# Fourier filter and gated convolution on one core: mixing by three real products for a pair of tiles, and the 64-point transform back in float32 quarters

## The chip, the cores and the metric

The kernel runs on one core of one Trainium2 chip. The core has a matrix engine (TensorE, PE in the profile, with its weight loads as PEld), a vector engine (VectorE, DVE), a scalar engine (ScalarE, ACT), GpSimd (POOL), and queues of DMA transfers that SyncE (SP) issues here. The metric is the device time of one execution in microseconds. A profiled execution has a span, from its first to its last instruction, and a time of its own, a little longer.

## The reference

```python
X = np.fft.rfft(x, axis=1)                 # x: 8 x 3200 x 256
Yr = Xr @ w_r - Xi @ w_i + b_r             # w_r, w_i: 256 x 256
Yi = Xr @ w_i + Xi @ w_r + b_i
Y = soft_threshold(Yr, 0.01) + 1j * soft_threshold(Yi, 0.01)
y = np.fft.irfft(Y, n=3200, axis=1)
gate = sigmoid(causal convolution of y, 5 taps per channel)
out = (gate * (y @ w_val)) @ w_out         # w_val, w_out: 256 x 256
```

The two sums Yr and Yi are a complex product of each frequency's 256 channels with a 256 x 256 matrix. They are called the mixing below.

## The kernel before

The 3200 positions are taken as 64 x 50, so that the long transform becomes a 50-point transform (p1 in the code), a 64-point one with its twiddles (s2), the mixing, the soft threshold, the 64-point transform back (s1i) and the 50-point transform back (s2i). Between p1 and s2, and between s1i and s2i, the data go to DRAM and come back in another layout. Then, for eight blocks of a batch, the gated convolution follows: value product v, five taps and the sigmoid, gate, output product o.

After s2 a batch has 25 tiles of 128 frequencies' real and imaginary parts. They are worked on in 12 pairs and a last single tile (u counts them, 13 for each batch). For a pair:

- s2 (L556) makes the spectrum of both tiles in PSUM (s, one buffer): float32 matmuls with the constants f2.
- ACT copies it to the type fp32r, which PE multiplies in one pass (L566, high part); DVE subtracts that from the spectrum (L568, low part); ACT negates the imaginary half (L571). So xs holds a high and a low part of [-Xi, Xr, Xi].
- The mixing (L591, L592) sums, for each of the two tiles, 2 halves of the channels x 3 products of high and low parts x 2 (real matrix, imaginary matrix) = 12 matmuls of 128 x 128 by 256 columns in PSUM (y_ps, one buffer): 24 for the pair.
- DVE adds the bias (L607, yb), ACT and DVE apply the threshold (L612, L614, tp), ACT and DVE split the result in high and low parts again (r_hl, by the helper at L311 and L313).
- s1i (L639) transforms back by 3 matmuls a tile, in fp32r with split constants g1, to PSUM (z_ps, one buffer of its own); ACT copies that (L646) and SP stores it.

The 50-point transforms (p1 at L517, y_p at L693) are float32 matmuls in four 64 x 64 quarters of PE, which run side by side.

What the engines do when is fixed ahead of time. Every step is added to a plan with an engine, an assumed duration, what it reads and writes, and a due time: `at` plus an offset from the table O. The plan (class Plan) is a list scheduler: it takes, piece by piece, the one of earliest due time among those that could begin soonest, with assumed costs for a change between quarters and full-width work (SWITCH) and a bound on the buffers of each kind (SLOTS). The result is one fixed order on each engine's queue. PSUM is given out by SLOTS too: one buffer each for the spectrum, the mixing and z, and two of two banks (ps_2), which p1, s2i, v and o share.

Of the kernel before, what the change touches and what calls it, by code (L numbers as in the profile page):

```python
# [32 lines left out]
def dft_constants():  # L33
# [46 lines left out]
class Plan:  # L80
# [11 lines left out]
    def add(self, at, engine, busy, fn, uses=(), sets=(), new=None, delay=None, quarters=False, kb=0, chain=None):  # L92
# [10 lines left out]
        p = dict(n=n, at=at, engine=engine, busy=busy, fn=fn, before=before, new=new or {}, quarters=quarters, kb=kb,  # L103
# [7 lines left out]
    def order(self):  # L111
# [25 lines left out]
        in_quarters, wire = False, 0.0  # L137
# [13 lines left out]
        while len(done) < len(pieces):  # L151
            best = None
            for e in engines:
# [56 lines left out]
SWITCH = 88  # L210
# [11 lines left out]
def act(n, kind="copy"):  # L222
# [36 lines left out]
def fourier_filter_then_gated_conv(ctx: ExitStack, tc: tile.TileContext, x, w_r, w_i, b_r, b_i,  # L259
# [57 lines left out]
    def load_matrix(at, name, w, dst):  # L317
# [52 lines left out]
    def load_matrix64(at, name, w, dst, uses=()):  # L370
# [23 lines left out]
    def load_g1(at, part):  # L394
        t = slice(part * 5, part * 5 + 5)
        key = ("st_g1", part)
        n = 5 * P

        def load():
            st = room(key, "g_hl", n).rearrange("p (t q) -> p t q", t=5)  # L400
            nc.sync.dma_start(out=st, in_=g1[:, t, :])
        add(at, "SP", 400, load, STORED, [key + (0,)], {key: "g_hl"}, kb=320)
        split(at + 0.01, n, ("g1", part), lambda: tl[key][:, 0:n].rearrange("p (t q) -> p t q", t=5),
              lambda: g1_sb[:, 0, t, :], lambda: g1_sb[:, 1, t, :], [key + (0,)])

    def load_bias(at):

        def load():
            for k, rows in ((0, N1), (1, N1 + 1)):
                for lo, hi, b in ((0, rows, b_r), (rows, P, b_i)):  # L410
                    nc.sync.dma_start(out=bias_sb[lo:hi, k, :],
                                      in_=b.rearrange("(o d) -> o d", o=1).to_broadcast([hi - lo, D]))
        add(at, "SP", 2200, load, STORED, [("bias", 0, 0)], kb=256)

    def load_bias_rows(at):
        key = ("b_hl", 0)
        v = lambda k: tl[key].rearrange("p (a d) -> p a d", a=2)[:, k, :]
        hl = split(at, D, key, lambda: bias_sb[:, 0, :], lambda: v(0), lambda: v(1), [("bias", 0, 0), ("a_dram", B - 2, 7)], {key: "tp"},
                   lambda: room(key, "tp", 2 * D, F32R))

        def rows():
            nc.vector.memset(f32(bias_hl[:, :]), 0.0)
            for row, k in ((0, 0), (32, 1), (64, 0), (96, 1)):
                nc.vector.tensor_copy(out=bias_hl[row:row + 1, :], in_=f32(v(k)[row:row + 1, :]))
            nc.vector.memset(f32(sel_sb[:, :]), 0.0)
            for row in range(0, P, 32):
                nc.vector.memset(f32(sel_sb[row:row + 1, row // N1 * N1:row // N1 * N1 + N1]), 1.0)
        add(at + 0.01, "DVE", 2500, rows, [*hl, ("a_dram", B - 2, 7)], [("bias_hl", 0, 0)])
# [463 lines left out]
```

## Time and profile before

| | us |
|---|---|
| median of 3 runs (lowest, highest) | 937.63 (937.32, 938.09) |
| the profiled execution's own time | 938.27 |
| its span | 936.5 |
| PE busy | 901.2 |
| weight loads (PEld) busy | 806.0 |
| DVE busy | 739.3 |
| ACT busy | 671.5 |

An engine's busy time is the union of its instructions' records. PE's records overlap, since matmuls are pipelined, so a busy PE says that it was never out of work, and not how long one matmul takes; for that one reads from one start to the next. The granted clock of PE was 0.985 of full speed on average. The timelines and groups that the prediction uses are shown there. In all of them a float32 matmul has two records (and two weight loads), a matmul in fp32r one.

### The profile page before, as it was taken

The page shows a single profiled execution, that of the slowest core. Times are in us where ns is not written, and L with a number is a line of the kernel's source. Part 1 is how long each engine was busy: PE and PEld are TensorE (multiplying, and loading weights), DVE is VectorE, ACT ScalarE, POOL GpSimd, SP SyncE. Part 2 cuts the span into 40 slices and gives each one's busy share as a digit, 9 for nine tenths or more (in the row PEclk, how much of TensorE's full clock was granted, in tenths as well). Part 3 has the DMA queues.
Part 4 walks back from the last instruction along what each step waited for, and adds up shares of the span by engine and source line. Part 5 has one row for each costly group of instructions (what it writes and reads, how often), then busy time and mean ns, then how long its engine had stood idle before and what let it go on. Part 6 is the DMA issues. An engine that isn't in the chain of part 4 may idle for free.

```text
span 936.5 us, 23789 instructions
## 1 busy us (share of the span) xinstructions
PE 901.2 (96%) x9918; PEld 806.0 (86%) x9918; DVE 739.3 (79%) x1211; ACT 671.5 (72%) x1091; POOL 3.7 (0%) x8
## 2 busy tenths in 40 slices
PE   7799699999999999999999999999999999999897
PEld 2488678899889998999889998899988999999675
DVE  1155776889778896898787895989878988988896
ACT  1176467878778777878777786878777787776664
POOL 0000000000000000000000000000001000000000
PEclk9699899999999999999999999999999999999999
DMA  6687666745675357644676356653664444422612
GB/s 202 211 256 238 182 211 207 234 152 164 206 230 183 99 187 245 218 135 142 204 224 215 114 170 210 221 162 124 213 231 152 134 155 134 146 88 76 196 70 87
DMA packets 105232, 164.52 MB, mean 176 GB/s; under 512 B 10054, under 2 KB 78406, under 8 KB 105126
## 3 DMA queue, kind: packets, MB, share of 16 engines
q1 hardware_dynamic: 104166, 159.74, 53.6%
q10 hardware_dynamic: 960, 3.28, 1.0%
q8 instruction: 78, 1.28, 0.6%
q14 instruction: 28, 0.23, 0.1%
HBM read 84.34 MB, written 78.64 MB: 174 GB/s over the span
## 4 chain that ended last, share of the span: by engine, by line
PE 67%; DVE 21%; ACT 5%; DMA 4%; issue 2%; SPq 1%; ACTq 0%; DVEq 0%
PE y_ps L591 12%; PE y_ps L592 12%; DVE acc L754 10%; PE o_ps L725 10%; PE v_ps L725 9%; PE s L556 8%; PE z_ps L639 7%; PE y_p L693 5%; PE p L517 5%; DVE acc L766 2%; DVE gated L313 2%; DVE yb L607 2%; DMA x<-in_x 1%; DVE xs L568 1%; DVE y_hl L313 1%
## 5 line engine op out<-in xcount | busy, mean ns | idle before, releaser
L754 DVE SCALAR_TENSOR_TENSOR acc<-y_sb,cw_sb,acc 128x400 f32<-128x400 f32 x512 | 300.5, 632 | 4.4 <-ACT acc L751 3.8
L591 PE MATMUL y_ps<-wri_sb,xs 128*128 128x256 f32 x1200 | 296.4, 287 | 2.0 <-DVE yb L607 1.2
L592 PE MATMUL y_ps<-wri_sb,xs 128*128 128x256 f32 x1152 | 277.5, 281 | 5.9 <-ACT xs L571 5.9
L591 PEld LDWEIGHTS y_ps<-wri_sb,xs 128*128 128x128 f32 x1200 | 227.4, 189 | 11.0 <-issue 5.9
L592 PEld LDWEIGHTS y_ps<-wri_sb,xs 128*128 128x128 f32 x1152 | 218.9, 190 | 6.1 <-ACT xs L571 6.1
L725 PE MATMUL o_ps<-gated,wo_sb 128*128 128x400 f32 x756 | 151.2, 348 | 0.0
L725 PEld LDWEIGHTS o_ps<-gated,wo_sb 128*128 128x128 f32 x756 | 134.5, 188 | 2.8
L725 PE MATMUL v_ps<-y_hl,wv_sb 128*128 128x400 f32 x636 | 127.2, 346 | 0.7 <-ACT r_hl L311 0.7
L556 PEld LDWEIGHTS s<-f_sb,a 128*128 128x128 f32 x800 | 101.8, 193 | 26.1 <-DVE xs L568 11.6
L556 PE MATMUL s<-f_sb,a 128*128 128x128 f32 x800 | 112.1, 282 | 9.0 <-DVE xs L568 4.8
L725 PEld LDWEIGHTS v_ps<-y_hl,wv_sb 128*128 128x128 f32 x636 | 112.3, 188 | 0.9 <-ACT r_hl L311 0.9
L566 ACT CAST xs<-s 128x512 fp32r<-128x512 f32 (+1 forms) x104 | 59.1, 568 | 56.6 <-PE y_ps L592 39.4
L313 DVE TENSOR_TENSOR r_hl<-tp,r_hl 128x512 fp32r<-128x512 f32 (+1 forms) x103 | 68.6, 666 | 35.2 <-ACT r_hl L311 34.9
L639 PE MATMUL z_ps<-r_hl,g_sb 128*128 128x256 f32 x594 | 93.9, 290 | 0.5 <-DVE r_hl L313 0.2
L607 DVE TENSOR_TENSOR yb<-y_ps,bias_sb 128x512 f32<-128x512 f32 (+1 forms) x103 | 68.5, 665 | 32.4 <-PE y_ps L592 31.9
L639 PEld LDWEIGHTS z_ps<-r_hl,g_sb 128*128 128x128 f32 x594 | 80.5, 189 | 13.2 <-ACT gated L311 3.2
L612 ACT ACTIVATE tp<-yb,nlam 128x512 f32<-128x512 f32 (+1 forms) x103 | 72.5, 705 | 23.3 <-DVE yb L607 20.9
L764 ACT ACTIVATE acc<-acc 128x400 f32<-128x400 f32 x128 | 67.1, 536 | 29.6 <-DVE acc L754 29.1
L311 ACT CAST gated<-acc 128x800 fp32r<-128x800 f32 x63 | 54.3, 862 | 45.3 <-DVE acc L766 45.1
L568 DVE TENSOR_TENSOR xs<-s,xs 128x512 fp32r<-128x512 f32 (+1 forms) x104 | 69.2, 665 | 18.1 <-ACT xs L566 18.1
L614 DVE SCALAR_TENSOR_TENSOR tp<-yb,tp 128x512 f32<-128x512 f32 (+1 forms) x103 | 68.6, 666 | 18.6 <-ACT tp L612 18.5
L751 ACT ACTIVATE acc<-y_sb,cw_sb 128x400 f32<-128x400 f32 x128 | 75.8, 628 | 9.7 <-DVE gated L313 9.7
(70 smaller groups left out, 944.5 us busy)
## 6 DMA issues: line engine op xcount, KB each, us to landing
zl<-z_dram SPq DMA_DIRECT2D x128, 200.0 KB
out<-o SPq DMA_DIRECT2D x63, 400.0 KB
a<-a_dram SPq DMA_DIRECT2D x96, 256.0 KB
z_dram<-z_t SPq DMA_DIRECT2D x96, 256.0 KB
x<-in_x SPq DMA_DIRECT2D x120, 200.0 KB
a_dram<-s SPq DMA_DIRECT2D x120, 200.0 KB
x<-in_x ACTq DMA_DIRECT2D x8, 200.0 KB
f_sb<-in_f SPq DMA_DIRECT2D x5, 320.0 KB
```

The source lines that it names most:

```text
L313: add(at + 0.001, "DVE", dve(n), lambda: nc.vector.tensor_tensor(out=low(), in0=src(), in1=f32(high()), op=ALU.subtract), [*uses, hl[0]], ...
L556: nc.tensor.matmul(p[:, 2 * i + c, :], tl[ka][:, i, c * P:(c + 1) * P], f2_sb[:, t, :], start=True, stop=True)
L568: add(at + O["s2"] + 0.1, "DVE", dve(m * P), lambda: nc.vector.tensor_tensor(out=xs()[:, 0:m, 1, N1:], in0=tl[k2][:, 0:m, :], in1=f32(xs() ...
L591: nc.tensor.matmul(p[:, i, :], xr, wri_sb[:, 0, hw, c, :], start=k == 0, stop=False)
L592: nc.tensor.matmul(p[:, i, :], xi, wri_sb[:, 1, hw, c, :], start=False, stop=k == 5 and not late)
L607: nc.vector.tensor_tensor(out=buffer(kb, "yb", [P, 2, D])[:, 0:n], in0=tl[ky][:, 0:n], in1=b_, op=ALU.add)
L612: nc.scalar.activation(out=buffer(kt, "tp", [P, 2, D])[:, 0:n], in_=src()[:, 0:n], func=AF.Relu, bias=nlam)
L614: add(at + 0.2, "DVE", dve(n * D), lambda: nc.vector.scalar_tensor_tensor(out=tl[kt][:, 0:n], in0=src()[:, 0:n], scalar=LAM, in1=tl[kt][:, ...
L639: nc.tensor.matmul(p[:, i, :], g1_sb[:, hg, t, :], tl[kr][:, hr, i, :], start=k == 0, stop=k == 2)
L725: nc.tensor.matmul(p[:, e, 0:TB], w[:, hw, c, e * P:(e + 1) * P], src(hy, c), start=n == 0, stop=n == 5)
L751: nc.scalar.mul(block(acc(c)), y_at(k, c, 0), cw_sb[:, c, 0:1])
L754: nc.vector.scalar_tensor_tensor(out=block(acc(c)), in0=y_at(k, c, j), scalar=cw_sb[:, c, j:j + 1], in1=block(acc(c)), op0=ALU.mult, op1=A ...
```

## The change

Mixing. With K = (Xr + Xi) w_r the mixing becomes Yr = K - Xi (w_r + w_i) and Yi = K + Xr (w_i - w_r): three real products instead of four. Both tiles of a pair are put side by side, real parts of both in one block of 128 columns and imaginary parts in another, so that each product takes 2 x 3 matmuls for the pair: 6 for K (k_ps, L620), 12 for the other two (y_ps, L615), 18 instead of 24. The sum Xr + Xi (sx) is made in float32: ACT copies the imaginary part (L595), DVE adds the real part (L602); ACT and DVE split it (L606, L607). The spectrum itself is split as before (L599, L603), the negation goes. DVE adds the bias to K for both parts (L626), then adds the other two products (L629). The last single tile of a batch keeps the four products.

Transform back. The threshold's result tp is no longer split. s1i of a pair is 8 float32 matmuls of 64 x 64 quarters by 256 columns (L651), to a buffer of ps_2 and no longer to one of its own; the single tile takes one full-width float32 matmul (L644). g1 is laid out for it, loaded as it is, and no longer split at the start.

Order. The planner has costs for five kinds of changes on PE, and other offsets; a late pair of the last batch and its preparations are dropped; the assumed landing of two loads is later by 3 and 4 us.

```diff
-SWITCH = 88
+SWITCH = {"rq": 92, "fq": 174, "qr": 75, "qf": 75, "ff": 77}
-O = {'load_x': -2.458,
+O = {'load_x': -2.454,
...
-SLOTS = {"x": 3, "zl": 3, "y_hl": 2, "s1": 2, "r_hl": 2, "a": 3, "xs": 2, "xz": 1, "yb": 2, "tp": 2, "zst": 3,
-         "acc": 2, "g_hl": 2, "o": 2, "ps_s2": 1, "ps_y": 1, "ps_z": 1, "ps_2": 2, "a_dram": 2, "z_dram": 2}
+SLOTS = {"x": 3, "zl": 3, "y_hl": 2, "s1": 2, "a": 3, "xs": 2, "sx": 2, "xz": 1, "yb": 2, "tp": 2, "zst": 3,
+         "acc": 2, "g_hl": 2, "o": 2, "ps_s2": 1, "ps_y": 1, "ps_k": 2, "ps_2": 2, "a_dram": 2, "z_dram": 2}
...
+            add(at2, "ACT", act(D), imag, done, [kd_ + (0,)], {kd_: "sx"})
+            add(at2 + 0.001, "ACT", act(2 * D, "cast"), high, done, [kx + (0,)], {kx: "xs"})
+            add(at2 + 0.001, "DVE", dve(D), lambda: nc.vector.tensor_tensor(out=sx(), in0=spec()[:, :, 0], in1=sx(), op=ALU.add), done, [kd_ + (0,)])
+            add(at2 + 0.002, "DVE", dve(2 * D), lambda: nc.vector.tensor_tensor(
+                out=tl[kx][:, 512:1024], in0=tl[k2].rearrange("p a b -> p (a b)"), in1=f32(tl[kx][:, 0:512]), op=ALU.subtract),
+                [*done, kx + (0,)], [kx + (1,)])
+            add(at2 + 0.003, "ACT", act(D, "cast"), lambda: nc.scalar.copy(out=ss(0), in_=sx()), [kd_ + (0,)], [kx + (2,)])
+            add(at2 + 0.004, "DVE", dve(D), lambda: nc.vector.tensor_tensor(out=ss(1), in0=sx(), in1=f32(ss(0)), op=ALU.subtract),
+                [kd_ + (0,), kx + (2,)], [kx + (3,)])
...
-            for c in range(2):
-                for hx, hw in ((0, 0), (0, 1), (1, 0)):
-                    xr = xs()[:, 2 * i + c, hx, N1:]
-                    xi = tl[kq][:, c, hx, :] if last else xs()[:, 2 * i + c, hx, 0:P]
-                    nc.tensor.matmul(p[:, i, :], xr, wri_sb[:, 0, hw, c, :], start=k == 0, stop=False)
-                    nc.tensor.matmul(p[:, i, :], xi, wri_sb[:, 1, hw, c, :], start=False, stop=k == 5 and not late)
+                for r, m in ((1, 2), (0, 3)):
+                    for k, (c, hx, hw) in enumerate((c, *h) for c in range(2) for h in HL):
+                        nc.tensor.matmul(p[:, 1 - r, :], xm(hx, c, r), w_sb[:, m, hw, c, :], start=k == 0, stop=k == 5)
+            def mix_sum():
+                p = buffer(kk, "ps_k", [P, D])
+                for k, (c, hx, hw) in enumerate((c, *h) for c in range(2) for h in HL):
+                    nc.tensor.matmul(p, sm(hx, c), w_sb[:, 0, hw, c, :], start=k == 0, stop=k == 5)
+            def bias():
+                nc.vector.tensor_tensor(out=buffer(kb, "yb", [P, 2, D]), in0=tl[kk].rearrange("p (a d) -> p a d", a=1).to_broadcast([P, 2, D]),
+                                        in1=bias_sb[:, 0:2], op=ALU.add)
+            add(at + 0.2, "DVE", dve(2 * D), lambda: nc.vector.tensor_tensor(out=yb(), in0=tl[ky], in1=yb(), op=ALU.add), [ky + (0,)], [kb + (0,)])
...
-            rs = split(at + 0.21, n * D, kr, lambda: tl[kt][:, 0:n], lambda: tl[kr][:, 0, 0:n], lambda: tl[kr][:, 1, 0:n],
-                       [kt + (0,)], {kr: "r_hl"}, lambda: buffer(kr, "r_hl", [P, 2, 2, D], F32R))
...
-            for k, (hg, hr) in enumerate(((0, 0), (0, 1), (1, 0))):
-                nc.tensor.matmul(p[:, i, :], g1_sb[:, hg, t, :], tl[kr][:, hr, i, :], start=k == 0, stop=k == 2)
+            for r in range(2):
+                for i in range(2):
+                    for e in range(2):
+                        nc.tensor.matmul(p[e * HP:(e + 1) * HP, i, 0:D], g[i * HP:(i + 1) * HP, r, e * HP:(e + 1) * HP],
+                                         tl[kt][i * HP:(i + 1) * HP, r, :], start=r == 0, stop=r == 1)
```

Line numbers of the change (L595 to L656 and so on) are those of the kernel with the change.

More of the change, by code (lines that the diff above doesn't have):

```diff
@@ L90, in __init__, with add @@
         self.opened, self.last = {}, {}
-    def add(self, at, engine, busy, fn, uses=(), sets=(), new=None, delay=None, quarters=False, kb=0, chain=None):
+    def add(self, at, engine, busy, fn, uses=(), sets=(), new=None, delay=None, mode="r", kb=0, chain=None, extra=0):
         n = len(self.pieces)
@@ L136, in order @@
         free = {e: 0.0 for e in engines}
[L137 removed]
+        mode, wire = "r", 0.0
         done = []
@@ L394, in load_g1 @@
     def load_g1(at, part):
[L395 to L404, printed above, removed]
+        t = slice(part * 5 * P, (part + 1) * 5 * P)
+        add(at, "SP", 400, lambda: nc.sync.dma_start(out=g1_sb[:, t], in_=g1[:, t]), STORED, [("g1", part, 0)], kb=320)
     def load_bias(at):
         def load():
[L409 to L428, printed above, removed]
+            for k, lo, hi, b in ((0, 0, P, b_r), (1, 0, P, b_i), (2, 0, N1 + 1, b_r), (2, N1 + 1, P, b_i)):
+                nc.sync.dma_start(out=bias_sb[lo:hi, k, :], in_=b.rearrange("(o d) -> o d", o=1).to_broadcast([hi - lo, D]))
+        add(at, "SP", 2200, load, STORED, [("bias", 0, 0)], kb=384)
     def load_conv(at):
@@ L596, in p2, with mix @@
-        w = [("w", m_, h) for m_ in ("w_r", "w_i") for h in ("high", "low")]
-        for i in range(n):
-            add(at, "PE", 1404 + 117 * late, lambda i=i: mix(i), [*parts, *w, *([("bias_hl", 0, 0)] if late else [])],
-                [ky + (i,)] + ([("turn", "mix", u)] if b == 0 and i == 0 else []), {ky: "ps_y"} if i == 0 else None)
-        made = [ky + (i,) for i in range(n)]
-        if late:
-            src, us = (lambda: tl[ky]), made
-        else:
+            def mix():
+                p = buffer(ky, "ps_y", [P, 2, D])
+                for k, (c, hx, hw) in enumerate((c, *h) for c in range(2) for h in HL):
+                    nc.tensor.matmul(p[:, 0, :], xs()[:, c, hx, N1:], w_sb[:, 0, hw, c, :], start=k == 0, stop=False)
+                    nc.tensor.matmul(p[:, 0, :], tl[kq][:, c, hx, :], w_sb[:, 1, hw, c, :], start=False, stop=k == 5)
@@ L645, in keep @@
+        add(at + O["s1i"], "PE", 430 if last else 900, s1i, [kt + (0,), *gs], [kz + (0,)], {kz: "ps_2"}, mode="f" if last else "q")
         def keep():
-            nc.scalar.copy(out=buffer(ko, "zst", [P, 2, D])[:, 0:n], in_=tl[kz][:, 0:n])
+            nc.scalar.copy(out=buffer(ko, "zst", [P, 2, D])[:, 0:n], in_=tl[kz][:, 0:n, 0:D])
         def store():
```

204 lines of the change are left out of this document (107 added, 97 removed).

## The prediction

> **What bounds the kernel now.** I read the page's busy line and chain of waits first, then the table of windows for one batch.
>
> ```profile
> span 936.5 us, 23789 instructions
> PE 901.2 (96%) x9918; PEld 806.0 (86%) x9918; DVE 739.3 (79%) x1211; ACT 671.5 (72%) x1091; POOL 3.7 (0%) x8
> PE 67%; DVE 21%; ACT 5%; DMA 4%; issue 2%; SPq 1%; ACTq 0%; DVEq 0%
> ```
> Two rows of the chain in order of time (start, length):
>
> ```profile
> 434.83 2.73 DVE acc L754 x5
> 543.24 2.73 DVE acc L754 x5
> ```
> And the windows: the first batch, one steady batch, the busiest hundred microseconds of DVE, and the end:
>
> ```profile
> 100.00:200.00 100.00, 88.77 (x1062) 79.78 (x1062) 78.31 (x144) 68.98 (x114) 0.00 (x0) 0.97 0.68 208
> 434.83:543.24 108.41, 108.29 (x1246) 100.33 (x1245) 89.49 (x147) 84.46 (x138) 0.00 (x0) 1.00 0.58 183
> 700.00:800.00 100.00, 98.68 (x1233) 94.97 (x1231) 87.87 (x141) 75.95 (x126) 3.07 (x2) 1.00 0.48 150
> 877.20:930.00 52.80, 47.81 (x581) 36.04 (x572) 49.78 (x82) 34.28 (x55) 0.00 (x0) 1.00 0.31 103
> ```
> The columns after the window's length are PE, PEld, DVE, ACT, POOL, PE clock, DMA share, GB/s. The same piece of the chain returns 108.4 us later: that is one batch, and seven follow each other this way. In it PE stands still for 0.1 us at clock 1.00 while DVE works 89.5 us (82.5%): PE's order sets the pace. The last 59 us are taps on DVE, after the last transform back, and the change leaves their order alone. The first batch (100 to 200) loses 11.2 us.
>
> **What the pieces on PE cost.** A busy PE overlaps its own records, so I take start to next start. Timeline of PE, stretches inside one steady batch or its like; columns: start, length, line, tiles.
>
> ```profile
> 414.00 0.61 PE L556 MATMUL s<-f_sb,a 128*128 128x128 f32 x4
> 414.36 0.36 PE L591 MATMUL y_ps<-wri_sb,xs 128*128 128x256 f32 x1
> 414.56 0.28 PE L592 MATMUL y_ps<-wri_sb,xs 128*128 128x256 f32 x1
> ...
> 451.33 1.05 PE L556 MATMUL s<-f_sb,a 128*128 128x128 f32 x8
> 452.14 0.36 PE L591 MATMUL y_ps<-wri_sb,xs 128*128 128x256 f32 x1
> ...
> 462.15 0.87 PE L639 MATMUL z_ps<-r_hl,g_sb 128*128 128x256 f32 x6
> 462.95 1.95 PE L517 MATMUL p<-x,f_sb 50*64 50x512 f32 x16
> 464.82 1.16 PE L556 MATMUL s<-f_sb,a 128*128 128x128 f32 x8
> 465.74 0.36 PE L591 MATMUL y_ps<-wri_sb,xs 128*128 128x256 f32 x1
> ...
> 482.92 0.86 PE L639 MATMUL z_ps<-r_hl,g_sb 128*128 128x256 f32 x6
> 483.62 0.28 PE L591 MATMUL y_ps<-wri_sb,xs 128*128 128x256 f32 x1
> ...
> 488.41 1.09 PE L517 MATMUL p<-x,f_sb 50*64 50x512 f32 x8
> 489.32 1.10 PE L693 MATMUL y_p<-g_sb,zl 50*64 50x50 f32 x64
> 490.35 0.97 PE L639 MATMUL z_ps<-r_hl,g_sb 128*128 128x256 f32 x6
> 491.16 0.28 PE L591 MATMUL y_ps<-wri_sb,xs 128*128 128x256 f32 x1
> ...
> 493.95 2.35 PE L725 MATMUL v_ps<-y_hl,wv_sb 128*128 128x400 f32 x12
> 496.14 1.05 PE L556 MATMUL s<-f_sb,a 128*128 128x128 f32 x8
> 497.12 1.95 PE L517 MATMUL p<-x,f_sb 50*64 50x512 f32 x16
> 499.00 0.98 PE L639 MATMUL z_ps<-r_hl,g_sb 128*128 128x256 f32 x6
> 499.81 0.28 PE L591 MATMUL y_ps<-wri_sb,xs 128*128 128x256 f32 x1
> ```
> Call single-pass 128-wide work R (mixing, z, v, o), float32 128-wide F (s), float32 quarters Q (p, y_p). Float32 shows two records a matmul. Mixing: 24 matmuls from 491.16 to 493.95, 0.116 us each. z of a pair: 0.70 (482.92). s: 0.36 for one tile, 0.81 for two, so 0.09 for following itself. p: 0.91 (488.41). y_p: 1.03 before z, of which 0.06 is for leaving Q (two p before z take 1.88), so 0.97. Changes of kind: F to Q 0.17 (0.98 at 496.14 against 0.81); Q to R 0.17 (the 0.06, and z 0.81 against 0.70); Q to F 0.17 (the 0.06, and s 0.92 at 464.82); R to Q 0.10 (z 0.80 at 462.15); F to R 0.08 (0.20 from 414.36).
>
> **The change on PE.** The mixing of a pair shrinks from 24 matmuls to 18, for 96 pairs: 576 x 0.116 = -67.0 us. The transform back of a pair becomes eight quarter matmuls of 256 columns: 512 columns for each quarter, as p, with twice its matmuls. From p (4 matmuls, 512 columns, 0.91) and y_p (32, 400 columns a quarter, 0.97) I solve 0.009 us a matmul and 1.7 ns a column; that makes 0.95. Without any cost for a matmul it is 0.87. I take 0.93, near p's row: 96 x 0.23 = +22.1, ends -5.8 and +1.9 from there. Single tiles and the dropped late pair add some 0.5. On PE, in the middle of the program, before:
>
> ```order
> L592 MATMUL y_ps<-wri_sb,xs 128x256
> L725 MATMUL o_ps<-gated,wo_sb 128x400 x12
> L556 MATMUL s_6078<-f_sb,a 128x128 x4
> L517 MATMUL p_6087<-x,f_sb 64x512 x4
> L693 MATMUL y_p<-g_sb,zl 64x50 x32
> L639 MATMUL z_ps<-r_hl,g_sb 128x256 x6
> L591 MATMUL y_ps<-wri_sb,xs 128x256
> ```
> and now (k_ps is the shared product):
>
> ```order
> L651 MATMUL z_ps<-tp,g_sb 64x256 x8
> L502 MATMUL p_4710<-x,f_sb 64x512 x4
> L703 MATMUL y_p<-g_sb,zl 64x50 x32
> L545 MATMUL s_4760<-f_sb,a 128x2x64 x2
> L620 MATMUL k_ps<-w_sb,xs 128x256 x6
> L735 MATMUL o_ps<-gated,wo_sb 128x400 x12
> L545 MATMUL s_4760<-f_sb,a 128x2x64 x2
> L615 MATMUL y_ps<-w_sb,xs 128x256 x12
> ```
> z has moved to the other quarter work, and s is cut in two. Counted along both orders, neighbours of different kind go F to Q from 26 to 21, Q to F 30 to 84, F to R 97 to 177, R to Q 47 to 94, Q to R 43 to 31: 29.3 us becomes 46.8, +17.5. Pairs of s in one go fall from 93 to 16: 77 x 0.09 = -6.9. Sum on PE: -67.0 + 22.1 + 0.5 + 17.5 - 6.9 = **-33.8 us**.
>
> **The change on DVE and ACT**, from the groups by form:
>
> ```profile
> L313 DVE TENSOR_TENSOR r_hl<-tp,r_hl 128x512 fp32r<-128x512 f32 x95 | 65.2, 687 | 35.2 <-ACT r_hl L311 34.9
> L607 DVE TENSOR_TENSOR yb<-y_ps,bias_sb 128x256 f32<-128x256 f32 x8 | 3.3, 418 | 0.3 <-PE y_ps L592 0.3
> L571 ACT ACTIVATE xs<-xs 128x512 fp32r<-128x512 f32 x96 | 60.0, 625 | 9.7 <-DVE xs L568 9.4
> L311 ACT CAST r_hl<-tp 128x512 fp32r<-128x512 f32 x95 | 59.0, 621 | 11.4 <-DVE tp L614 10.9
> L566 ACT CAST xs<-s 128x512 fp32r<-128x512 f32 x96 | 56.1, 585 | 49.1 <-PE y_ps L592 35.6 <-PE s L556 13.4
> L566 ACT CAST xs<-s 128x256 fp32r<-128x256 f32 x8 | 3.0, 371 | 7.5 <-PE y_ps L592 3.8 <-PE s L556 3.7
> ```
> From the timelines of DVE (two neighbours in a steady batch) and of PE (its first s):
>
> ```profile
> 502.94 0.69 DVE L607 TENSOR_TENSOR yb<-y_ps,bias_sb 128x512 f32<-128x512 f32 x1
> 503.56 0.69 DVE L568 TENSOR_TENSOR xs<-s,xs 128x512 fp32r<-128x512 f32 x1
> ```
> ```profile
> 38.90 1.52 PE L556 MATMUL s<-f_sb,a 128*128 128x128 f32 x8 [3.55 <-DMA a<-a_dram]
> ```
> Each pair loses the low part of r_hl and gains a second addition of 512 (yb): even, as long as an addition that reads PSUM beside SBUF costs what L607 costs now. It also gains two operations of 256 (the sum sx, and its low part). Such a record is 0.42 long; neighbours' records overlap by 0.07 (0.69 long, the next one begins 0.62 later), so one costs between 0.35 and 0.42. I take 0.38: 12 pairs x 2 x 0.38 = +9.1 us a batch, 98.6 in all. ACT loses 1.25 us a pair (L571, L311) and gains two operations of 256, 0.74: it gets 0.5 lighter and stays off the path. The DMAs of a steady batch are the same ones in the same queue, so they cost nothing here; they have to keep up with a batch that is 4% shorter, at a share of 0.58. At the start the casts of g1 go, and two sums of the weights with their high and low parts come in: six operations of 512 on DVE, 6 x 0.62 = 3.7 us. They lie ahead of the first s, where PE waits 3.55 us for its first a; without that cover they would cost those 3.7. On DVE, a pair of tiles in a steady batch before, with what each instruction waits for:
>
> ```order
> L568 TENSOR_TENSOR xs<-s_6864,xs 128x4x128 [waits Activation_49]
> L607 TENSOR_TENSOR yb<-y_ps,bias_sb 128x512
> L754 SCALAR_TENSOR_TENSOR acc<-y_sb,cw_sb,acc 128x400 [waits DVE_49] x3
> L614 SCALAR_TENSOR_TENSOR tp<-yb,tp 128x512 [waits Activation_49]
> L754 SCALAR_TENSOR_TENSOR acc<-y_sb,cw_sb,acc 128x400 [waits DVE_49] x2
> L313 TENSOR_TENSOR r_hl<-tp,r_hl 128x512 [waits Activation_49]
> ```
> and now (yb is first made from the shared product, then the other two are added):
>
> ```order
> L626 TENSOR_TENSOR yb<-k_ps,bias_sb 128x512 [waits PE_49]
> L602 TENSOR_TENSOR sx<-s_5324,sx 128x256 [waits PE_49,Activation_49]
> L603 TENSOR_TENSOR xs<-s_5324,xs 128x512
> L607 TENSOR_TENSOR xs<-sx,xs 128x256 [waits Activation_49]
> L629 TENSOR_TENSOR yb<-y_ps,yb 128x512 [waits PE_49]
> L764 SCALAR_TENSOR_TENSOR acc<-y_sb,cw_sb,acc 128x400 x2
> L635 SCALAR_TENSOR_TENSOR tp<-yb,tp 128x512 [waits Activation_49]
> ```
> The wait of r_hl's low part on ACT (L313) is gone. A new one stands at L602: L603 needs ACT's cast of s and has no wait of its own, so L602's wait already covers that cast, and the sum sx starts behind it. Queued behind L602 are L603, which frees the single PSUM buffer of s for the next pair, L607, for which the shared product waits, and L629, which frees y_ps; PE comes to stand when they are late by more than the o or v piece (2.2 us) between. The Trainium skill ("PSUM — Partial Sum Buffer", section on bank collisions) says that two engines must not read one bank at once, which would force this; no run here shows a collision. Without that rule the first rival below would lose its price.
>
> **Sum.** 936.5 - 33.8 = 902.7. But DVE would be busy 98.6 of some 104 us (108.4 less 33.8 / 8), 95%. Where DVE reached 87.9% (700 to 800), PE already stood still 1.3%; I take that share as the new stall, 7 batches x 104 x 1.3% = +9. Bounds: 0, and the rivals. The first batch's 11.2 us stay: DVE still converts w_val in one block there. Span 911.7; the profiled execution took 938.27, 1.8 above its span, and the median 937.63 is 0.6 below that: **913 us**.
>
> **Rivals.** *DVE stands at L602.* If it arrives early each time, it loses up to a cast, 0.585 x 12 = 7.0 us a batch: 98.6 + 7.0 = 105.6, with the 1.3% 107.0. Seven batches gain 1.4 each, the first one keeps its 33.8 / 8 = 4.2: 14 in all, span 922.5, time 924. For it: L313's 34.9 us of waiting for ACT now. Against: DVE's queue holds other work ahead of L602, so that the cast is mostly over when it gets there.
> *DVE becomes the bound, and it is slower.* The steady batch breaks even at 98.6 / 108.4 = 91% of DVE busy. If 87.9% is all that it reaches beside a full PE, since in its fixed order it waits for ACT and PE in turn, a batch takes 112.2: 3.8 x 7 - 4.2 = +22, 960. For it: no stretch of a hundred microseconds shows more, and these waits are many and short. Against: from 877 to 930, where its taps are what the end waits for, DVE works 94% (49.78 of 52.80); and most of its 17.5% idle time in a steady batch was time for which nobody waited.
> *z waits for ps_2.* It now shares the two slots of p, y_p, v, o; z, p, y_p in a row need z's copy (0.58, the 512 form above) done within p's 0.91, which fits. If each z waited 0.35 us, the gain would be gone: 938. The Trainium skill ("TensorEngine Tiling (Array Packing)", section PSUM Bottleneck) warns that emptying PSUM limits after such a step.
> *More than forecast.* No new stall and the first batch's idle time gone: 902.7 - 11.2 + 1.1 = 893.
>
> **How the numbers follow.** Forecast 0.64 (895 to 922), DVE at L602 0.14 (922 to 937), DVE the bound 0.10 (slower), ps_2 0.05 (around 938), more 0.07. Range 895 to 933: the forecast, most of the first rival, a little of ps_2. A measurement here tells 0.2% (1.9 us) from no change: faster 0.86, same 0.04, slower 0.10.
>
> **What would show it.** In the profile after: z pieces of 0.87 to 0.95 start to start; a batch of 104 to 106 us; DVE busy 92 to 95% of it and PE idle about 1%, with DVE as the releaser; L602's idle time before it below 20 us in all; a first batch that still loses some 11 us, and a last stretch of 59 us as before. Wrong if PE idles over 3% of a steady batch with DVE as releaser, if L602 shows 30 us or more behind ACT, or if z takes over 1.0.

## The result, and the profile after

The changed kernel takes **917.07 us** (median of 4 runs, 916.56 to 917.74); the kernel before, run beside it on the same chip, 937.62 us (937.32 to 938.09). The ratio is 0.9781, with a 95% interval of 0.9764 to 0.9798. The profiled execution took 916.63 us, 1.8 above its span of 914.8.

First the page of the changed kernel: span, busy line and the chain of waits by engine.

```profile
span 914.8 us, 24904 instructions
PE 865.0 (95%) x10294; PEld 727.4 (80%) x10294; DVE 792.1 (87%) x1385; ACT 627.6 (69%) x1080; POOL 3.8 (0%) x8
PE 53%; DVE 32%; DMA 6%; ACT 4%; issue 3%; SPq 0%; ACTq 0%; DVEq 0%
```

TensorE works 36.2 us less than the 901.2 of before. The span shrank by only 21.7, so TensorE's idle time grew from 35.3 to 49.8 us. DVE works 52.8 us more, and its share of the chain went from 21 to 32%.

Two rows of the chain in order of time (start, length), the same piece one batch apart:

```profile
531.57 2.46 PE o_ps L735 x12
634.97 2.44 PE o_ps L735 x12
```

This batch takes 103.4 us; the one shown of before took 108.4. Batches differ by a few per cent. Counted from one single tile to the next (DVE's cast to xz, L570, before L578), the five batches between 207 and 730 us take 103.4 to 105.4 us, 104.5 on average; five of before take 106.9 to 109.5, 108.2 on average. The one shown is the shortest. The windows of the changed kernel: that batch, then the start, the first batch, the steady batches, and the end. The columns are those of the windows before (length; PE, PEld, DVE, ACT, POOL; granted clock, DMA share, GB/s).

```profile
531.57:634.97 103.40, 102.87 (x1291) 90.56 (x1291) 96.60 (x169) 79.19 (x137) 0.00 (x0) 1.00 0.60 192
0.00:43.00 43.00, 28.24 (x87) 9.05 (x87) 8.99 (x11) 7.51 (x9) 0.67 (x6) 0.88 0.57 186
43.00:160.00 117.00, 99.86 (x986) 77.04 (x990) 77.68 (x159) 58.80 (x110) 0.00 (x0) 0.94 0.74 223
160.00:780.00 620.00, 612.56 (x7697) 539.36 (x7690) 583.23 (x1012) 471.87 (x814) 3.14 (x2) 1.00 0.58 186
856.00:915.00 59.00, 50.39 (x579) 36.96 (x570) 50.28 (x83) 35.15 (x55) 0.00 (x0) 0.99 0.31 105
```

The same windows of the kernel before, as far as they were not shown:

```profile
0.00:43.00 43.00, 31.25 (x99) 11.66 (x100) 7.37 (x8) 7.59 (x9) 0.67 (x6) 0.80 0.60 195
43.00:160.00 117.00, 106.48 (x960) 93.05 (x962) 73.89 (x133) 73.46 (x119) 0.00 (x0) 0.96 0.74 226
160.00:780.00 620.00, 616.90 (x7115) 574.01 (x7106) 523.46 (x850) 484.54 (x792) 3.07 (x2) 1.00 0.57 181
```

The length less PE's busy time is its idle time. Of the 14.5 us of idle time that TensorE gained, 3.0 lie in the start (14.8 against 11.8), 6.6 in the first batch (17.1 against 10.5), and 4.3 in the steady batches (7.4 against 3.1). The last stretch is 59 us, as it was.

The first 160 us hold most of the loss. The start, from the timeline of the changed kernel (behind a row in brackets: the idle time just before it, and what ended it):

```profile
27.50 1.23 DVE L472 COPY s<-p 128x1024 f32<-128x1024 f32 x1 [9.07 <-DMA a_dram<-s]
27.58 1.01 ACT L472 COPY s<-p 128x1024 f32<-128x1024 f32 x1 [9.31 <-DMA a_dram<-s]
28.65 3.82 PE L467 MATMUL p<-x,f_sb 50*64 50x512 f32 x16 [7.17 <-ACT s L472]
42.97 1.34 PE L545 MATMUL s<-f_sb,a 128*128 128x128 f32 x8 [4.62 <-DMA a<-a_dram]
```

The copies of the third block of the start wait until the second block's stores have left their staging slot. With r_hl gone, the second block's tag became g_hl, which is the third block's too. TensorE then stands behind these copies, and the first s comes at 42.97 instead of 38.90. And in the first batch, PE's longest wait, now (first row) and before (second row):

```profile
121.12 2.08 PE L545 MATMUL s<-f_sb,a 128*128 128x128 f32 x8 [6.26 <-DVE xs L561]
109.67 0.58 PE L592 MATMUL y_ps<-wri_sb,xs 128*128 128x256 f32 x1 [5.85 <-ACT xs L571]
```

From 111 to 121 us DVE converts the weights of the values and the taps in one block, and PE's next s waits for a low part that is queued behind it. The kernel before had such a wait behind the same block (101.6 to 108.3 us) and lost almost as much. What the first batch lost in addition lies ahead of the block. From the first s to the block's first instruction, before and now:

```profile
38.90:101.58 62.68, 60.96 (x476) 52.78 (x477) 31.98 (x48) 39.96 (x64) 0.00 (x0) 0.95 0.77 239
42.97:111.18 68.21, 60.65 (x526) 45.78 (x527) 38.13 (x69) 34.64 (x65) 0.00 (x0) 0.95 0.80 239
```

PE's idle time there went from 1.7 to 7.6 us, 5.8 of the 6.6. It is made of ten waits of 0.3 to 2.1 us for the steps by which ACT and DVE split the spectrum and for yb and tp. DVE is busy for only 56% of this stretch.

### The profile page after: what moved, and what is told of

Same layout as the page of the kernel before. It is cut to its first block, busy times and chain, and to the rows that moved or that the text cites. A ratio compares the mean times of both kernels' runs of the same rounds, so it can differ in the third digit from the quotient of the medians.

```text
span 914.8 us, 24904 instructions
## 1 busy us (share of the span) xinstructions
PE 865.0 (95%) x10294; PEld 727.4 (80%) x10294; DVE 792.1 (87%) x1385; ACT 627.6 (69%) x1080; POOL 3.8 (0%) x8
## 4 chain that ended last, share of the span: by engine, by line
PE 53%; DVE 32%; DMA 6%; ACT 4%; issue 3%; SPq 0%; ACTq 0%; DVEq 0%
DVE acc L764 13%; PE y_ps L615 9%; PE o_ps L735 8%; PE s L545 8%; PE v_ps L735 8%; PE z_ps L651 6%; PE k_ps L620 5%; PE y_p L703 4%; DVE acc L776 4%; DVE gated L310 3%; PE p L502 3%; DVE xs L603 2%; DMA f_sb<-in_f 2%; DVE yb L629 2%; DVE yb L626 2%
## 5 line engine op out<-in xcount | busy, mean ns | idle before, releaser
L615 PE MATMUL y_ps<-w_sb,xs 128*128 128x256 f32 x1152 | 155.4, 283 | 3.5 <-DVE xs L603 1.9
L615 PEld LDWEIGHTS y_ps<-w_sb,xs 128*128 128x128 f32 x1152 | 145.0, 188 | 9.0 <-ACT xs L599 3.1
L651 PE MATMUL z_ps<-tp,g_sb 64*64 64x256 f32 x1536 | 104.5, 387 | 2.3 <-DVE tp L635 1.3
L620 PE MATMUL k_ps<-w_sb,xs 128*128 128x256 f32 x576 | 91.5, 294 | 0.5 <-DVE xs L607 0.3
L703 PEld LDWEIGHTS y_p<-g_sb,zl 50*64 50x64 f32 x4096 | 67.1, 135 | 18.5 <-ACT z_t L656 7.7
L626 DVE TENSOR_TENSOR yb<-k_ps,bias_sb 128x512 f32<-128x512 f32 x96 | 66.3, 691 | 17.4 <-PE k_ps L620 17.2
L620 PEld LDWEIGHTS k_ps<-w_sb,xs 128*128 128x128 f32 x576 | 75.6, 190 | 5.4 <-issue 2.7
L703 PE MATMUL y_p<-g_sb,zl 50*64 50x50 f32 x4096 | 70.5, 219 | 6.4 <-issue 2.6
L656 ACT COPY z_t<-z_ps 128x512 f32<-128x512 f32 (+1 forms) x104 | 58.9, 566 | 24.4 <-PE z_ps L651 22.3
L651 PEld LDWEIGHTS z_ps<-tp,g_sb 64*64 64x64 f32 x1536 | 50.7, 132 | 29.3 <-issue 4.2
```

Of the source, the lines that this page charges most:

```text
L615: nc.tensor.matmul(p[:, 1 - r, :], xm(hx, c, r), w_sb[:, m, hw, c, :], start=k == 0, stop=k == 5)
L620: nc.tensor.matmul(p, sm(hx, c), w_sb[:, 0, hw, c, :], start=k == 0, stop=k == 5)
L626: nc.vector.tensor_tensor(out=buffer(kb, "yb", [P, 2, D]), in0=tl[kk].rearrange("p (a d) -> p a d", a=1).to_broadcast([P, 2, D]), in1=bias ...
L651: nc.tensor.matmul(p[e * HP:(e + 1) * HP, i, 0:D], g[i * HP:(i + 1) * HP, r, e * HP:(e + 1) * HP], tl[kt][i * HP:(i + 1) * HP, r, :], star ...
L703: nc.tensor.matmul(pv[h][e * HP:(e + 1) * HP, c, m, :], zt[half(h), m, c * P + e * HP:c * P + (e + 1) * HP], g2_sb[half(h), :], start=True ...
```

## The experiments

Each ratio is to the kernel before, run beside it on the same chip; the changed kernel's own is 0.9781 (0.9764 to 0.9798).

### The start's slot

```diff
-        tag = ("s1", "g_hl", "g_hl", "s1")[v]
+        tag = ("s1", "xs", "g_hl", "s1")[v]
```

> Alone the staging slot of the second block of the start is changed: the third block's copies get a slot of their own instead of the one that the second block's stores have to leave first. Theory (the start lost its 4.07 us, first spectrum matmul at 42.97 against 38.90 us, to that slot, and nothing behind it hides it): the copies of line 472 lose most of their 9.07 and 9.31 us of waiting, the first spectrum matmul comes at 39 us, and the time falls by 3 to 4.5 us against the changed kernel, to 912.5 to 914. Rival (the first batch is held by VectorE's blocks anyway, so that an earlier start only lengthens the waits between 43 and 130 us): the first spectrum matmul comes at 39 us all the same, but the time stays within 1 us of 917.

Measured: 914.14 us, ratio 0.9739 (0.9703 to 0.9775). Once more, with more executions:

> The start's slot alone once more, in more rounds: the first measurement (0.9739 of before, 0.9703 to 0.9775) overlaps that of the changed kernel (0.9781, 0.9764 to 0.9798). Theory (the start's 4 us come through, less what the first batch eats): 0.9725 to 0.9760. Rival (the first batch eats all of it): 0.977 or more.

Measured: 914.89 us, ratio 0.9757 (0.9732 to 0.9781). The timeline of the first of the two:

```profile
23.44 1.01 ACT L472 COPY s<-p 128x1024 f32<-128x1024 f32 x1 [4.98 <-DMA a_dram<-s]
26.43 1.23 DVE L472 COPY s<-p 128x1024 f32<-128x1024 f32 x1 [4.71 <-DMA a_dram<-s]
38.77 2.04 PE L545 MATMUL s<-f_sb,a 128*128 128x128 f32 x8 [5.33 <-DMA a<-a_dram]
```

The waits of about 9 us shrink to 5, and the first s comes 4.2 us earlier: the slot was the cause of the late start. What arrives at the end is less, 2 to 4 us by the two ratios, and both intervals overlap that of the changed kernel: a gain over it is likely, but not settled. Over the kernel before it is. In the profile the lead is down to 1.5 us at the second batch's first s (119.58 against 121.12). The four microseconds in which the changed kernel waits are worked by this one at half the clock (first row). The other two rows go from the first s to the second batch's first s, in the changed kernel and in this one:

```profile
39.00:43.00 4.00, 3.67 (x14) 2.13 (x16) 1.26 (x3) 1.26 (x3) 0.00 (x0) 0.50 0.80 211
42.97:121.12 78.15, 64.32 (x565) 48.20 (x565) 47.42 (x98) 37.13 (x69) 0.00 (x0) 0.94 0.80 235
38.77:119.58 80.81, 68.42 (x564) 51.07 (x564) 47.25 (x98) 37.13 (x69) 0.00 (x0) 0.90 0.75 228
```

The same matmuls keep PE busy 4.1 us longer at the lower clock (0.90 against 0.94), while PE idles 1.4 us less (12.4 against 13.8). So in these two executions it is the clock that eats the lead, and not the waits of the first batch, as the rival had it.

### The first batch: order, place, or sum of DVE's work

Three kernels move the conversions. One spreads the 13 steps of each conversion (values, taps, output). Due times count pairs of tiles, some 8 us each, so 1.0 is a pair, and not a microsecond as the expectation has it; in the trace the steps for the values run from 114 to 125 us, those for the output weights from 141 to 159.

```diff
-            add(at + 0.0001 * k, "DVE", busy, piece, uses, done, new if k == 0 else None, delay=busy + (130 if k == 12 else 0))
+            add(at + 1.0 * k, "DVE", busy, piece, uses, done, new if k == 0 else None, delay=busy + (130 if k == 12 else 0))
```

> Alone the due times of the 13 conversion steps of the weights of the values and taps lie 1.0 us apart instead of 0.0001, so that VectorE does other work of the first batch between them. Theory (the block of conversions at 111 to 121 us costs TensorE the 6.26 us for which it waits at 121.12, and TensorE sets the pace): the 6.26 us shrink to under 2 and the time falls by 4 to 6 us, to 911 to 913. Rival (VectorE's sum of work in the first batch, not its order, holds TensorE there): the idle time turns up in other waits before 160 us and the time stays within 1.5 us of 917.

Measured: 917.91 us, ratio 0.9785 (0.9758 to 0.9812): no change, as the rival said. The 6.26 us are gone as one wait, but waits of 2.0, 2.4 and 3.3 us stand at 119, 126 and 150 us, and TensorE idles 17.2 us between 43 and 160, as it did.

Two move the loads and conversions forward, on top of the start's slot:

```diff
-        if u == 7:
+        if u == 2:
             load_matrix64(u + 0.1, "w_val", w_val, wv_sb)
-        if u == 8:
+        if u == 5:
             load_conv(u + 0.1)
-        if u == 9:
+        if u == 6:
             load_matrix64(u + 0.1, "w_out", w_out, wo_sb, [("w", "w_val", "low")])
```

> The third block of the start gets a staging slot of its own, and the loads and conversions of the late weights come with pairs 2, 5 and 6 of the first batch instead of 7, 8 and 9, into the stretch up to 80 us where VectorE is 40 to 60% busy; nothing is left out. Theory (the first batch loses its time to VectorE's sum of work after 100 us, which can be laid into VectorE's idle stretch before): the wait of 6.26 us goes and another 3 to 6 us come back beside the 3 of the start: 906 to 911 us. Rival (the conversions cost TensorE the same wherever they lie, or their loads collide with the transfers up to 80 us, 87% busy): 913 us or more.

Measured: 915.46 us, ratio 0.9755 (0.9731 to 0.9779). The other one has 3, 7 and 8 in these places:

> As the kernel with the early conversions, but with pairs 3, 7 and 8: a smaller step. Theory: between the start's slot alone (about 913) and the earlier placing, 907 to 912 us. Rival: 913 us or more, no better than the start's slot alone.

Measured: 918.78 us, ratio 0.9806 (0.9780 to 0.9832). Neither beats the start's slot alone: the rival holds. In the profile of the earlier placing the conversions run at 79 to 87, 101 to 104 and 111 to 119 us, and the waits on PE have moved with them:

```profile
86.63 2.50 PE L615 MATMUL y_ps<-w_sb,xs 128*128 128x256 f32 x10 [3.82 <-DVE xs L603]
119.14 1.19 PE L545 MATMUL s<-f_sb,a 128*128 128x128 f32 x4 [8.28 <-ACT xs L606]
```

The last kernel of this group takes the work out, in the same order:

```diff
-                fn()
+                if n < 2 * D or k in (6, 7):
+                    fn()
```

> In the order of the changed kernel 11 of the 13 conversion steps of the two late weight matrices (values and output) are left out, so that sign, exponent and low word of these weights are not built: some 6 us less on VectorE in each of two places of the first batch, at 111 and at 137 us. Theory (what TensorE loses in the first batch is VectorE's sum of work there, not its order): the waits of 6.26 and 2.85 us go or shrink below 2 together, and the time falls by 5 to 10 us, to 907 to 912. Rival (something else stands behind these waits: the loads, ScalarE's casts, or the order): 915 or more.

Measured: 912.18 us, ratio 0.9708 (0.9676 to 0.9740), 5 us below the changed kernel by the medians, 7 by the ratios. Its window of the first batch:

```profile
43.00:160.00 117.00, 106.45 (x1115) 81.31 (x1116) 73.34 (x148) 64.79 (x121) 0.00 (x0) 0.96 0.79 239
```

TensorE idles 10.6 us there instead of 17.1, so the conversions cost PE 6.5 us; in the three other places tried they cost about the same. Moving them to another engine was not tried. The waits ahead of the conversions are not their doing. From the first s to the first step of conversion this kernel has

```profile
43.50:112.19 68.69, 61.20 (x526) 46.13 (x527) 38.13 (x70) 34.53 (x65) 0.00 (x0) 0.94 0.81 239
```

which is 7.5 us of idle time on PE, as in the changed kernel (7.6).

### Three products or four, and the order numbers

The mixing with four products again, in the pair layout and with the quarters (w_n is then the negative of w_i, and w_d, sx and the sum of the two product tiles fall away):

```diff
-                for r, m in ((1, 2), (0, 3)):
-                    for k, (c, hx, hw) in enumerate((c, *h) for c in range(2) for h in HL):
-                        nc.tensor.matmul(p[:, 1 - r, :], xm(hx, c, r), w_sb[:, m, hw, c, :], start=k == 0, stop=k == 5)
+                for o, ms in ((0, (0, 2)), (1, (1, 0))):
+                    n_ = 0
+                    for c in range(2):
+                        for hx, hw in HL:
+                            for r in range(2):
+                                nc.tensor.matmul(p[:, o, :], xm(hx, c, r), w_sb[:, ms[r], hw, c, :], start=n_ == 0, stop=n_ == 11)
+                                n_ += 1
...
-            add(at + O["mix_sum"], "PE", 702, mix_sum, [kx + (2,), kx + (3,), *w("w_r")], [kk + (0,)] + ([("turn", "mix", u)] if b == 0 else []), {kk: "ps_k"})
-            add(at, "PE", 1404, mix, [kx + (0,), kx + (1,), *w("w_n", "w_d")], [ky + (0,)], {ky: "ps_y"})
+            add(at, "PE", 2808, mix, [kx + (0,), kx + (1,), *w("w_r", "w_i", "w_n")], [ky + (0,)] + ([("turn", "mix", u)] if b == 0 else []), {ky: "ps_y"})
```

> The mixing goes back to four products (24 matmuls a pair in one piece instead of 6 and 12; no sum of the spectrum's halves, no sum of the two product tiles: per pair VectorE does 0.33 + 0.33 + 0.60 us less, ScalarE one copy and one cast less); the pair layout, the transform back in quarters and the order numbers stay as they are changed. Theory (TensorE's order sets the pace, 0.116 us a mixing matmul): 576 matmuls more are +67, some 96 entries into the mixing fewer are -8 to -15, and some 3 to 8 of the stalls go with VectorE's lighter load: 957 to 975 us. Rival (the changed kernel's batch is held by VectorE, 93% busy, as much as by TensorE, so that giving VectorE 121 us of work back returns a good part): under 950 us.

Measured: 967.19 us, ratio 1.0315 (1.0288 to 1.0341). Its steady batch:

```profile
490.09:601.23 111.14, 111.14 (x1364) 98.99 (x1363) 84.11 (x134) 72.25 (x113) 0.00 (x0) 1.00 0.56 179
```

72 matmuls more at 0.116 us make 8.4; the batch grew by 7.7, from 103.40 (by 7.0 on the average of five batches). The third product saved is worth 50 us of the whole here. Pair layout and quarters without it cost 29 us more than the kernel before: the prediction's terms without the mixing (22.1 + 0.5 + 17.5 - 6.9) make 33. DVE, with 12.5 us less of work a batch, returns 0.7 to 1.4 us a batch at most, and the changes of kind that went with k_ps are in that too: TensorE does not stand still at all.

The changed kernel's work by the old table of order numbers:

```diff
-SWITCH = {"rq": 92, "fq": 174, "qr": 75, "qf": 75, "ff": 77}
+SWITCH = {"rq": 88, "fq": 88, "qr": 88, "qf": 88}
...
-     'p3': 3.595,
-     'load_z': -1.358,
+     'p3': 3.054,
+     'load_z': -0.892,
...
```

> The changed kernel's work, with the table of order numbers of the kernel before (the new piece, the sum of the mixing, keeps its number) and the planner's one price of 88 ns for every change of kind on TensorE. Theory (the gain is work that left TensorE; the table only trims changes of kind and stalls): 917 to 930 us, still faster than before. Rival (the gain depends on the new table, without it the waits for VectorE eat what the work gave): 931 us or more.

Measured: 928.21 us, ratio 0.9889 (0.9864 to 0.9914). Still faster than before; the table is worth 11 us. That lead is there already at the end of the first batch's transform back: the first copy into y_sb ends 11.5 us later (at 167.2 against 155.7). A steady batch is 104.1 us, near the changed kernel's average of 104.5.

### Which engine holds the steady batch

Four kernels in the order of the changed one. Less of DVE's taps:

```diff
+            if j == 1 and b < B - 1:
+                s_ = lambda v: v[:, :, 0:N2]
+                nc.vector.scalar_tensor_tensor(out=s_(block(acc(c))), in0=y_at(k, c, j)[:, :, 0:N2], scalar=cw_sb[:, c, j:j + 1],
+                                               in1=s_(block(acc(c))), op0=ALU.mult, op1=ALU.add)
+                return
```

> In the order of the changed kernel the first of the taps that VectorE adds runs on 100 of 400 columns in all batches but the last (16 instructions a batch; the rest of that tap is left out): about 0.31 us less for each, 5 us less VectorE work a batch, 35 in all, on an engine that is 93% busy. Theory (TensorE sets the pace, VectorE has room): only what is left of TensorE's waits for it can come back, 1 to 6 us, so 911 to 916. Rival (VectorE sets the pace together with TensorE): 15 to 35 us come back, under 902.

Measured: 914.23 us, ratio 0.9749 (0.9719 to 0.9779), which overlaps that of the changed kernel. Less of TensorE's transform back:

```diff
-            for r in range(2):
+            for r in range(1):
...
-                                         tl[kt][i * HP:(i + 1) * HP, r, :], start=r == 0, stop=r == 1)
+                                         tl[kt][i * HP:(i + 1) * HP, r, :], start=True, stop=True)
```

> In the order of the changed kernel the transform back of a pair is done with the real half alone (4 quarter matmuls instead of 8; the imaginary half of the sum is left out): about 0.45 us less on TensorE for each of 96 pairs, 43 us in all, 5.4 a batch; VectorE's and ScalarE's work stays. Theory (TensorE sets the pace until VectorE's 96.6 us of the 103.4 fill the batch): the batch falls to 98 to 99.5 us, 876 to 891 us in all. Rival (VectorE's order holds the batch already): it stays over 101 us, 900 us or more.

Measured: 912.54 us, ratio 0.9726 (0.9701 to 0.9750). My theory had promised 26 to 41 us; 4.5 came. More work on DVE:

```diff
-            add(at2 + 0.004, "DVE", dve(D), lambda: nc.vector.tensor_tensor(out=ss(1), in0=sx(), in1=f32(ss(0)), op=ALU.subtract),
+            add(at2 + 0.004, "DVE", dve(D), lambda: [nc.vector.tensor_tensor(out=ss(1), in0=sx(), in1=f32(ss(0)), op=ALU.subtract) for _ in range(2)],
```

> In the order of the changed kernel the low part of the sum of the spectrum's halves (line 607) is computed twice: 96 instructions of 0.33 us more on VectorE, 32 us in all, 4 a batch, and nothing else. Theory (VectorE has 6.8 us of a steady batch free): the steady batch grows by 0 to 1.5 us, the first batch by up to 3, 919 to 929 us. Rival (no room on VectorE): nearly all of the 32 us shows, 942 us or more.

Measured: 955.21 us, ratio 1.0186 (1.0154 to 1.0217): all of the 32 us and 6 more. So the theory that TensorE alone holds the batch fell, and a new one had to stand against both reliefs at once (the first two diffs together):

> Both reliefs at once, in the order of the changed kernel: the shortened first tap (VectorE 5 us a batch less) and the half transform back (TensorE 5.4 us a batch less); the rest of that tap and the imaginary half are left out. Apart they gave about 2 and 4 us of the whole time and left the batch at 102.9 and 102.0 of 103.4 us. Theory now (TensorE and VectorE hold the batch alike, each within 1.5 us of the other, so that relief of one is worth next to nothing): together the batch falls to 97 to 99 us and the time to 876 to 892 us. Rival (neither: the handing to and fro between the engines, or the transfers, holds the batch near 102): 900 us or more.

Measured: 889.04 us, ratio 0.9475 (0.9450 to 0.9501), inside the 876 to 892; the batch fell to 99.8 us, and not to 97 to 99. A steady batch of each, from the windows, in this order: short tap, half back, both, double low part.

```profile
468.99:571.91 102.92, 102.70 (x1292) 90.55 (x1292) 92.45 (x168) 78.83 (x137) 0.00 (x0) 1.00 0.59 193
```
```profile
460.51:562.53 102.02, 98.67 (x1196) 86.65 (x1196) 96.54 (x169) 78.32 (x137) 0.00 (x0) 1.00 0.60 194
```
```profile
453.97:553.79 99.82, 98.30 (x1196) 86.73 (x1196) 91.87 (x169) 78.28 (x137) 0.00 (x0) 1.00 0.61 199
```
```profile
484.84:593.62 108.78, 105.12 (x1295) 91.95 (x1294) 101.63 (x182) 78.52 (x137) 0.00 (x0) 0.98 0.57 183
```

The first row gives TensorE's floor: with DVE at ease PE is idle for 0.2 us, and the batch is 102.9. The second gives DVE's: with 4.2 us less on PE, PE idles 3.3 us, and the batch is still 102.0, of which DVE works 96.5, or 94.6%. That DVE sets this second floor is shown by the third row: with DVE's work cut as well, the same work on PE takes 99.8. The changed kernel, at 103.40, lies 0.5 above the one floor and 1.4 above the other (its batch one earlier, at 104.3, lies 1.4 and 2.3 above them). That is why either relief alone is worth 3 to 5 us of the whole, and both together 28. In the fourth row DVE stands at 93.4% of a longer batch: with more work its share of a steady batch does not rise. This is no limit of the engine: from 160 to 260 us of the same execution DVE works 96.5%. It is what this order of work reaches in a steady batch.

What keeps DVE from 100%, in the batch of the half transform back (waited for: us in total, times, longest):

```profile
DVE tp L635 <- ACT tp L633: 1.6, 2, 0.8
DVE yb L629 <- PE y_ps L615: 1.3, 2, 0.9
DVE y_hl L310 <- ACT y_hl L308: 0.9, 1, 0.9
DVE sx L602 <- ACT xs L599: 0.7, 1, 0.7
DVE yb L626 <- PE k_ps L620: 0.6, 1, 0.6
DVE acc L776 <- PE v_ps L735: 0.2, 1, 0.2
```

These eight waits make 5.3 of its 5.5 idle us. Each is a handover in the fixed order for which DVE came up to 0.9 us early; none is long. What PE waits for in that batch is DVE's product with the gate (1.1 us), which frees a slot of ps_2, and ACT's copy of z (2.2 us), which frees one too.

## Why the prediction was right, and where its steps were off

The forecast was 913 us, the time 917.07, inside the range of its likeliest case. That it came within 4 us is luck in part: PE's work and the stalls of the steady batches came out some 7 us better than forecast, the start and the first batch some 10 us worse, and the two nearly cancel. Its steps:

**PE's work: -33.8 forecast, -36.2 measured** (901.2 to 865.0 busy). The prices held. PE's timeline in the steady batch of the changed kernel:

```profile
543.26 1.57 PE L615 MATMUL y_ps<-w_sb,xs 128*128 128x256 f32 x12
544.76 1.09 PE L651 MATMUL z_ps<-tp,g_sb 64*64 64x256 f32 x16
545.67 1.04 PE L502 MATMUL p<-x,f_sb 50*64 50x512 f32 x8
546.64 0.71 PE L545 MATMUL s<-f_sb,a 128*128 128x128 f32 x4
547.11 0.95 PE L620 MATMUL k_ps<-w_sb,xs 128*128 128x256 f32 x6
547.90 0.61 PE L545 MATMUL s<-f_sb,a 128*128 128x128 f32 x4
548.26 2.42 PE L735 MATMUL v_ps<-y_hl,wv_sb 128*128 128x400 f32 x12
```

Start to start, z takes 0.91 (forecast 0.93, of 0.87 to 0.95). The twelve mixing matmuls take 1.50: 12 x 0.116 is 1.39, so the change from R to Q costs 0.11 (forecast 0.10). p takes 0.97 ahead of s, 0.06 over its 0.91, and s takes 0.47 behind it, where a lone s behind k_ps takes 0.36: Q to F costs 0.17, as forecast. k_ps ahead of s takes 0.79; 6 x 0.116 is 0.70, so 0.09 are paid around it (F to R was forecast at 0.08). What makes the remaining 2.4 us was not broken down.

**DVE: 98.6 us a batch forecast, 96.6 measured.** The operations of 256 were priced at 0.38. From DVE's timeline of the changed kernel:

```profile
67.02 0.42 DVE L602 TENSOR_TENSOR sx<-s,sx 128x256 f32<-128x256 f32 x1
67.36 0.68 DVE L603 TENSOR_TENSOR xs<-s,xs 128x512 fp32r<-128x512 f32 x1
67.96 0.41 DVE L607 TENSOR_TENSOR xs<-sx,xs 128x256 fp32r<-128x256 f32 x1
68.29 0.68 DVE L626 TENSOR_TENSOR yb<-k_ps,bias_sb 128x512 f32<-128x512 f32 x1
```

Start to start they take 0.34 and 0.33, below the end of 0.35 that I had put on them. That is 1.1 of the 2.0 us. DVE's share of the batch is 93.4%, as forecast (92 to 95).

**New stalls: +9 forecast, +4.3 measured** in the steady batches (160 to 780 us). They are 104.5 us on average, as forecast (104 to 106), the one shown 103.4. The step was right in that the batch stands 0.5 us above PE's floor and 1.4 above DVE's, and too large: I took the share from one window of before. DVE as the releaser, which I had named as its sign, shows for only 1.2 of PE's 7.4 idle us; 1.9 end with ACT's copy of z, and for 3.1 the profile shows no releaser.

**The start: nothing forecast beyond the hidden sums, +4.1 measured.** This step failed. The sums of the weights do lie under PE's wait for the first a, as I wrote. What I did not read is the changed tag of the second block's staging slot, which stands in the full diff and not in the part shown above: a slot shared with the next block makes that block's copies wait for stores. With its own slot the first s comes at 38.77.

**The first batch: "some 11 us stay", +6.6 measured.** Here the term was mis-sized: it was taken over from before, as if the conversions alone made it. They cost about what they did (waits of 6.26 now and 5.85 before). What came in addition, 5.8 of the 6.6, are the short waits in the pairs ahead of them, which the kernel without the conversions has too. The new steps lengthen the way from one spectrum to the next: the single buffer of s is now read by four operations in turn (L595, L599, L602, L603) and no longer by two, and PE waits 2.05 us for it at the second pair (46.36) where it waited 1.40 before (41.82). That this explains all of these waits is argued from the timeline; no run tests it. The new table of order numbers is not the cause. The window of the kernel with the old table shows 19.7 us of idle time:

```profile
43.00:160.00 117.00, 97.31 (x793) 73.55 (x794) 72.57 (x148) 54.36 (x102) 0.00 (x0) 0.90 0.74 213
```

**The rivals.** *DVE stands at L602* did not come. In the waits of the changed kernel (us in total, times, longest) it has

```profile
DVE sx L602 <- ACT xs L599: 27.4, 19, 8.0
```

of which 8.0 lie before the very first pair, 15.2 in the rest of the first 160 us and 4.2 from 160 to 780; the changed kernel's steady batch has 0.7. The total lies above the 20 us I had named and below the 30 that would have decided. The Trainium skill ("PSUM — Partial Sum Buffer", section on bank collisions) says that two engines must not read one bank at once. Whether that is why the sum stands behind ACT's cast, no run shows: none shows a collision, and none lets both read.

*DVE becomes the bound* came closest to being true. It said that DVE in its fixed order cannot fill a batch, and put its ceiling at 87.9%, the most that the profile of before showed; it breaks even at 91%. The most that a steady batch of any run shows is 94.6%, and the doubled low part shows what more work on DVE then costs: 955 us. With the 96.6 us of work that it turned out to be, a batch breaks even at 96.6 / 108.4 = 89%.

*z waits for ps_2* came only in small, and not at z. The group of z on PE (busy us, mean ns, idle before it) shows 2.3 us of idle time in all, and most of that is for DVE's tp, not for a buffer:

```profile
L651 PE MATMUL z_ps<-tp,g_sb 64*64 64x256 f32 x1536 | 104.5, 387 | 2.3 <-DVE tp L635 1.3
```

It is the pieces behind z that pay: from 160 to 780 us o_ps and y_p wait 1.9 us in all for ACT's copy of z, and with the half transform back, where a z takes half as long, the pieces behind it wait 6.9 us from 300 to 700. The Trainium skill warns that the copy out of PSUM may become the bottleneck after a fourfold speedup of TensorE by tiling ("TensorEngine Tiling (Array Packing)", section PSUM Bottleneck). Here a z became slower on PE (0.91 for 0.70), so this case is not that one; the 1.9 and 6.9 us point the same way.

## What to carry to other kernels

When a change lightens the engine that sets the pace and loads the next one, ask how full the second one can get in its fixed order, not only how full it will be: here it was 94.6% of a steady batch, and the result stood 1.2 points below it. Relieving one of two engines that stand this close tells little about the other; relieve both before you conclude that something else holds the batch. A stretch that loses time before the change can lose more after it, even where the work that you blame for the loss is the same: look at each wait in it. And read the small edits of a diff, such as a staging tag, as you read the large ones: each shared slot is a wait.

## What was not expected of the hardware

A quarter matmul in float32 with half the columns costs half: eight of 256 columns (z, 0.91 us) take as long as four of 512 (p, 0.91 before, and here 0.97 with the 0.06 for leaving Q). The 0.009 us that I had put on each matmul do not show at 256 columns. At 50 columns they may: 32 matmuls of y_p, 400 columns a quarter, still take 0.97 (152.46 to 153.43 in the kernel with the start's slot).

The clock granted to TensorE varies in the first 160 us: 0.88 in the start and 0.94 in the first batch of the changed kernel, 0.80 and 0.96 in the kernel before, and 0.50 in the four microseconds that the mended start fills. From 160 to 780 us it is 1.00 in both. An early microsecond of TensorE work is thus not worth a microsecond in every execution. Two profiled executions of the kernel with the start's slot show it, with spans of 914.5 and 919.4 us. They are level at the second batch's first s (119.58 and 119.66). PE's next wait of over 2 us ends with these rows, of the one and the other:

```profile
143.40 1.13 PE L545 MATMUL s<-f_sb,a 128*128 128x128 f32 x8 [2.85 <-ACT xs L606]
143.82 2.05 PE L545 MATMUL s<-f_sb,a 128*128 128x128 f32 x8 [2.83 <-ACT xs L606]
```

The same eight records take 1.13 us in the one and 2.05 in the other, and from 145 to 151 us the granted clock is 1.00 in the one and 0.50 in the other. By the first copy into y_sb they are 4.2 us apart (153.68 and 157.91), most of the 4.9 between the spans. Over all executions this kernel's times spread from 911.8 to 917.0 and from 912.4 to 921.2 us in its two measurements, against 916.6 to 917.7 for the changed kernel.
